# Delta-rule attention and two MoE layers on one core: both halves of each attention stage together, TensorE held in program order, PSUM divided anew, sums stored in four transfers

## The chip, the core and the metric

One core of one Trainium2 chip runs the whole program. The metric is device microseconds of one execution, the median of the runs. Engines in the profile: PE is TensorE, DVE is VectorE, ACT is ScalarE, POOL is GpSimd, SP is SyncE, which here issues DMAs only. PSUM is the memory that PE writes; ACT and DVE read results out of it.

## The reference

Three layers one after the other. The first is a delta-rule attention: per batch and head a 48x48 state is read and corrected token by token over 768 tokens. Its output feeds two mixture layers on 3072 tokens.

```python
B, H, S, D = 4, 8, 768, 48
for t in range(S):
    y[:, :, t] = einsum('bhd,bhde->bhe', q[:, :, t], state)
    v_old = einsum('bhde,bhd->bhe', state, k_n[:, :, t])
    state = state + beta[:, :, t] * einsum('bhd,bhe->bhde', k_n[:, :, t], v[:, :, t] - v_old)
x = y.transpose(0, 2, 1, 3).reshape(3072, 384)
h = maximum(x @ w_in, 0); x = (h * h) @ w_out          # 384 -> 2048 -> 384
h = maximum(maximum(x @ w1, x @ w2), x @ w3)           # 384 -> 768
out = h @ w_out2                                       # 768 -> 384
```

## The kernel before

**Chunks.** The 768 tokens are cut into 12 chunks of 64. Within a chunk the recursion is written as products of small matrices and one triangular inverse per head and batch; from chunk to chunk only the state `Sb` is carried. Each matrix product with float32 weights is done as three products of a high and a low part (`xh`, `xl`; `gh`, `gl`; `win_h`, `win_l`).

**Main loop.** Before it stands a prologue (Gram products and the inverses of the first two chunks). Then 12 rounds follow, one for each chunk `c`. In round `c`, `moe_a(c)` does the first mixture layer of chunk `c`: eight groups `s1` (18 matmuls into `p`, 2 PSUM buffers, then relu and square on ACT, the cast `gh` on ACT and the difference `gl` on DVE) and eight groups `s2` (12 matmuls into `px`). `s2` of a group stands two groups behind its `s1`, so that the last two `s2` groups close the round. The columns of `px` beyond the 384 sums also take a part of the attention's sums. At the end two DVE transposes bring `px` to SBUF as `xs`, and DMAs on SP's queue store it to `x2_d[c]`, eight for each chunk.

**Woven in.** `steps` takes a step of other generators between the steps of `moe_a`, each at a rate of its own: `attention(c+1)`; `kkps` in rounds 1, 3, 5, 7 (Gram products of two later chunks: PE `pk`, `pq`, DVE mask products, stores `kk`, `p` on SP's queue); `solve32` in rounds 0, 2, 4, 6, 8 (a load `buf<-kk`, then a chain of some 60 vector operations on DVE from `ss` at L247 over the pairs L268 and L270 to L271, which inverts two chunks' triangles; `norm` transposes a factor on PE as `pt`).

**Attention.** The 16 pairs of batch and head pair are split in two halves `p` = 0 and 1. For each half: `st0` multiplies `v` by `normT` (L419), forms `pA` and `pY` from the state and takes `r = v - pA` (L434); `zz` and `ww` (both halves at once, `pZ`, `pW`) finish the inverse; `mm_u` gives `pU`, copied to `u`; `st2` gives the output `pY` and the state's growth `pD` (then `Sb`), copied to `yy`; `st3` transposes `yy` on PE (`pT`) to `xh` and `xl` of chunk c+1. All of these matmuls address quarters or sixteenths of the array (64x64, 48x64 or 32x32), while `p` and `px` use 128x128.

**Order.** The kernel is written with Tile: a scheduler orders every engine's instructions by its own model of times from the order in which they are emitted, their dependences, and extra ordering edges (`behind`). The program of PE is therefore not in the order of the code; the split stages that the next section but one shows are the scheduler's. Phase 3 (the second mixture layer, from 655.46 us) follows the last round.

## Time and profile before

| what | value |
|---|---|
| runs | 960.38, 962.7, 967.49 us, median 962.7 us |
| profiled execution | 961.26 us, of which the span of the profile 959.5 us and 1.76 us around it |
| PE busy | 892.2 us, 93% of the span |
| DVE, ACT, POOL busy | 470.4, 409.2, 149.3 us |
| rounds 0 to 11 | 80.20 to 655.46 us |
| phase 3 | 655.46 to 959.5 us |

The profiled execution lies 1.4 us under the median. Times in the views are counted from the start of the span. A round begins where its first `p` matmul begins.

### The profile page before, as it was taken

To read this page: it belongs to the slowest core of one execution; us is meant where nothing else is said; L and a number is where in the kernel's file an instruction comes from. 1 tells how busy PE (TensorE), PEld (TensorE's weight loads), DVE (VectorE), ACT (ScalarE), POOL (GpSimd) and SP (SyncE) were. 2 spreads that over 40 slices of the span, in tenths; PEclk is the share of its full clock that TensorE was granted. 3 is DMA by queue.
4 is the path that set the end of the run, shared out by engine and by line. 5 is a ranking of instruction groups with operands and counts; after the bars stand their busy time and mean duration, and the time that the engine had idled before them with its cause. 6 is when DMAs were issued, how large, how long until landed. Compare 5 with 4: busy or idle time off the path is not lost.

```text
span 959.5 us, 26517 instructions
## 1 busy us (share of the span) xinstructions
PE 892.2 (93%) x11422; PEld 855.0 (89%) x11422; DVE 470.4 (49%) x1048; ACT 409.2 (43%) x857; POOL 149.3 (16%) x245
## 2 busy tenths in 40 slices
PE   5438889889999999999999999999999999999998
PEld 4337778889999999999999999999999999999998
DVE  2978886249424942493258354466623323323221
ACT  1756854444454545444544466473422212212211
POOL 2351112310322142214211420001100000000000
PEclk8557979999999999999999999999999999999999
DMA  9977723571574156426532633234301100100000
GB/s 198 336 207 188 213 69 81 154 170 55 145 188 93 56 150 179 99 61 161 149 74 69 144 112 101 59 100 110 114 25 33 42 25 25 33 21 14 17 17 34
DMA packets 118309, 98.83 MB, mean 103 GB/s; under 512 B 76160, under 2 KB 98480, under 8 KB 118192
## 3 DMA queue, kind: packets, MB, share of 16 engines
q1 hardware_dynamic: 97408, 58.23, 23.3%
q0 software_dynamic: 11712, 32.41, 12.5%
q10 hardware_dynamic: 9072, 6.49, 2.3%
q8 instruction: 90, 1.47, 0.7%
q14 instruction: 27, 0.22, 0.1%
HBM read 72.45 MB, written 24.64 MB: 101 GB/s over the span
## 4 chain that ended last, share of the span: by engine, by line
PE 80%; DVE 11%; ACT 4%; DMA 3%; issue 2%; SPq 0%; ACTq 0%; DVEq 0%
PE p L909 23%; PE p L548 20%; PE px L566 18%; PE po L926 8%; DVE buf L270 3%; DVE buf L268 3%; PE pA L429 2%; PE pU L446 2%; PE pY L493 1%; DVE gl L555 1%; DMA buf<-kk 1%; PE pD L471 1%; PE pT L514 1%; PE pk L180 1%; PE pY L429 1%
## 5 line engine op out<-in xcount | busy, mean ns | idle before, releaser
L909 PE MATMUL p<-x_h,w 128*128 128x384 f32 x864 | 220.1, 336 | 0.0
L566 PE MATMUL px<-wout,gh 128*128 128x384 f32 x768 | 202.6, 343 | 2.6 <-ACT wout L126 1.2
L548 PE MATMUL p<-xh,win_h 128*128 128x256 f32 x576 | 168.7, 294 | 5.7 <-DVE gl L555 4.5
L548 PE MATMUL p<-xl,win_h 128*128 128x256 f32 x576 | 164.2, 288 | 1.5 <-DVE xl L518 1.3
L548 PE MATMUL p<-xh,win_l 128*128 128x256 f32 x576 | 164.3, 286 | 0.0
L909 PEld LDWEIGHTS p<-x_h,w 128*128 128x128 f32 x864 | 156.2, 188 | 0.1
L909 PE MATMUL p<-x_l,w 128*128 128x384 f32 x432 | 145.3, 336 | 0.0
L566 PEld LDWEIGHTS px<-wout,gh 128*128 128x128 f32 x768 | 135.6, 189 | 6.1 <-ACT wout L126 1.4
L555 DVE TENSOR_TENSOR gl<-p,gh 128x512 fp32r<-128x512 f32 x96 | 66.2, 689 | 143.0 <-ACT gh L554 143.0
L566 PE MATMUL px<-wout,gl 128*128 128x384 f32 x384 | 130.1, 339 | 0.0
L548 PEld LDWEIGHTS p<-xh,win_h 128*128 128x128 f32 x576 | 111.1, 193 | 9.7 <-issue 2.6
L548 PEld LDWEIGHTS p<-xl,win_h 128*128 128x128 f32 x576 | 110.8, 194 | 2.7 <-DVE xl L518 2.0
L548 PEld LDWEIGHTS p<-xh,win_l 128*128 128x128 f32 x576 | 111.5, 194 | 0.3
L552 ACT ACTIVATE p<-p 128x512 f32<-128x512 f32 x96 | 55.9, 582 | 130.1 <-PE p L548 128.8
L915 DVE TENSOR_TENSOR mx<-p,mx 128x384 f32<-128x384 f32 x48 | 26.7, 557 | 123.0 <-PE p L909 123.0
L909 PEld LDWEIGHTS p<-x_l,w 128*128 128x128 f32 x432 | 81.3, 188 | 0.0
L917 ACT CAST hh<-mx 128x384 fp32r<-128x384 f32 x48 | 24.6, 513 | 119.4 <-DVE mx L916 119.3
L566 PEld LDWEIGHTS px<-wout,gl 128*128 128x128 f32 x384 | 72.3, 188 | 0.8 <-DVE gl L555 0.2
L554 ACT CAST gh<-p 128x512 fp32r<-128x512 f32 x96 | 56.3, 587 | 17.1 <-PE px L566 14.7
L270 DVE TENSOR_TENSOR buf<-buf 128x30 f32<-128x30 f32 (+9 forms) x180 | 60.6, 337 | 5.5
L268 DVE TENSOR_TENSOR buf<-buf 128x30 f32<-128x30 f32 (+9 forms) x180 | 60.0, 333 | 5.5
L553 ACT ACTIVATE p<-p 128x512 f32<-128x512 f32 x96 | 55.9, 582 | 2.9
(183 smaller groups left out, 1372.0 us busy)
## 6 DMA issues: line engine op xcount, KB each, us to landing
kq<-in_kc_dram POOLq DMA_DIRECT2D x22, 448.0 KB, 4.9
raw<-in_moe_w_dram SPq DMA_DIRECT2D x18, 384.0 KB, 3.4
p<-p POOLq DMA_DIRECT2D x22, 256.0 KB, 3.2
raw<-in_moe_w_out_dram SPq DMA_DIRECT2D x13, 384.0 KB, 3.4
v<-in_vt_dram POOLq DMA_DIRECT2D x24, 192.0 KB, 4.5
ktp<-in_kt_dram POOLq DMA_DIRECT2D x24, 192.0 KB, 3.0
x<-xs SPq DMA_DIRECT2D x96, 48.0 KB, 2.6
out_dram<-os ACTq DMA_DIRECT2D x24, 192.0 KB, 1.9
```

The costliest lines, as they stand in the source:

```text
L268: eng.tensor_tensor(out=tv, in0=M[:, 0:j, j].unsqueeze(2).broadcast_to([u, j, m]), in1=M[:, j, j + 1:n].unsqueeze(1).broadcast_to([u, j, m ...
L270: yield eng.tensor_tensor(out=M[:, 0:j, j + 1:n], in0=M[:, 0:j, j + 1:n], in1=tv, op=ALU.add)
L429: j = pe.matmul(ps[half(t ^ i), u], kq_[feat(t), u, i], Sb[feat(t), U2 * p + u], start=not i or u == 0, stop=not i, skip_group_check=bool(i))
L548: pe.matmul(p1[:, j], w[:, k, f], x[c][:, k], start=n == 0 and j == 0, stop=n == 8, skip_group_check=True)
L552: act.activation(out=p1, in_=p1, func=AF.Relu)
L553: act.activation(out=p1, in_=p1, func=AF.Square)
L554: last_gh[0] = act.copy(gh, p1).ins
L555: last_gl[0] = vec.tensor_sub(out=gl, in0=p1, in1=gh.bitcast(F32)).ins
L566: g = pe.matmul(px[:, h, 0:DM], x[:, j, hs], w, start=f == 0 and i == 0, stop=f == NF - 1 and i == 2, skip_group_check=True)
L909: pe.matmul(p, w[i][:, k, fs], x[:, k], start=n == 0, stop=n == 8)
L915: vec.tensor_max(out=t, in0=ps[1], in1=t)
L926: pe.matmul(po[:, 0:DM], x[:, f, js], w[:, f], start=i == 0, stop=i == 17)
```

## The change

**Halves.** From chunk 1 on, each of `st0`, `mm_u`, `st2`, `st3` does both halves in one step, where a half had steps of its own; the rate of the attention's steps falls with their number. `load_att` of both halves of the next chunk is issued after `st2`.

**Order on PE.** From round 2 on, each matmul and transpose goes through `tc.keep_in_program_order`, so that the scheduler keeps PE's instructions in the order in which the code emits them.

**PSUM.** `ps_at` (for `pA`, `pU`, `pD`, `pZ`, `pW`, `pT`, Gram products) has 2 buffers where it had 3; `ps_y` (for `pY`) has 2 where it had 1. `r` is no tile of its own: the subtraction writes `v`. `yy` has 2 buffers.

**Copies.** For half 1 (all chunks but chunk 1) the copies of `u` and `yy` out of PSUM are put on DVE instead of ACT.

**Stores.** `store_sums` stores `xs` by four DMAs of twice the size, at the second `s1` group of the next round. `x2_d` gets an axis for the halves of a chunk's 256 tokens; phase 3 loads `xr` by 128 tokens (twelve DMAs for a block of 384 tokens instead of eight, each run of bytes half as long). The transposes to `xs` stay behind the last DVE copy of the attention.

**Numbers.** The step at which the inverse is put after its load (`landing`) is 14 in round 2; `norm` comes at step 24 instead of 12; the Gram products begin later.

```diff
-    ps_at = pp.enter_context(tc.tile_pool(name="ps_at", bufs=3, space=PSUM))
-    ps_y = pp.enter_context(tc.tile_pool(name="ps_y", bufs=1, space=PSUM))
+    ps_at = pp.enter_context(tc.tile_pool(name="ps_at", bufs=2, space=PSUM))
+    ps_y = pp.enter_context(tc.tile_pool(name="ps_y", bufs=2, space=PSUM))
...
+        def matmul(self, *a, **k):
+            i = nc.tensor.matmul(*a, **k)
+            return tc.keep_in_program_order(i) if self.ordered else i
...
-            r = fresh("r", p, 6, [128, U2, D])
-            vec.tensor_sub(out=r, in0=v, in1=pA)
+            vec.tensor_sub(out=v, in0=v, in1=pA)
...
+            on_vec = p and c != 1
+            def put(to, po):
+                if on_vec:
+                    last_vec[0] = vec.tensor_copy(to, po).ins
+                else:
+                    last_act[0] = act.copy(to, po).ins
...
-                    if p and not c:
+                    if p and c != 1:
                         last_vec[0] = vec.tensor_copy(yy[p][half(i), :, t], pY[half(1 - t), Q * i:Q * i + Q]).ins
...
-            order = ((st0, 0),), *(((),) if c in (4, 10) else ()), ((zz, (k21, x1)),), *(((),) if c == 1 else ()), ((ww, 0),), ((mm_u, 0),), ((st2, 0),), ((st0, 1), (st3, 0)), ((mm_u, 1),), ((st2, 1),), ((st3, 1),)
+            order = both(st0), ((zz, (k21, x1)),), *(((),) if c == 1 else ()), ((ww, 0),), both(mm_u), both(st2), both(st3)
...
-            vec.transpose(out=xs[:, h], in_=px[:, h, 0:DM])
-            for a in range(4):
-                nc.sync.dma_start(x2_d[c][:, :, 4 * h + a], xs[32 * a:32 * a + 32, h].rearrange("i (b j) -> i b j", j=32))
+            i = vec.transpose(out=xs[:, h], in_=px[:, h, 0:DM])
+            if last_vec[0]:
+                behind(i.ins, last_vec[0])
+        sums.append((c, xs))
...
+        c, xs = sums.pop()
+        for a in range(4):
+            nc.sync.dma_start(x2_d[c].rearrange("i h b a j -> a i (h b) j")[a], xs[32 * a:32 * a + 32].rearrange("i h (b j) -> i (h b) j", j=32))
...
-                if g and n == 12:
+                if g and n == (24 if g > 1 else 12):
                     norm(nm)
...
-                extra.append(((10 if c in (3, 9) else 9) / 15.0, attention(c + 1)) if c > 1 else (13 / 15.0, later(3, attention(1))) if not c else (16 / 15.0, later(5, attention(2))))
+                extra.append((6.8 / 15.0, attention(c + 1)) if c > 1 else (11 / 15.0, later(3, attention(1))) if not c else (14 / 15.0, later(6, attention(2))))
...
-                solve_next = solve32(SOLVE[c], landing=16 if c == 8 else 10) if c else solve32(1, (pool,) * 2)
+                solve_next = solve32(SOLVE[c], landing={2: 14, 8: 16}.get(c, 10)) if c else solve32(1, (pool,) * 2)
...
             if c == 2:
                 kc_after.clear()
+                pe.ordered = True
```

Three places show what becomes of the order. In the changed kernel every matmul has the line of the wrapper, L48.

PE in round 4, before: the products of `st2` of half 0 (`pY`, `pD`) in the middle, where an `s2` group stands between two parts of them.

```order
L471 MATMUL pD<-u,ktp_147 64x48 x2
L493 MATMUL pY<-u,p 64x48 x2
L566 MATMUL px<-wout_1069,gh 128x384 x2
L566 MATMUL px<-wout_1069,gl 128x384
L566 MATMUL px<-wout_1069,gh 128x384 x2
L566 MATMUL px<-wout_1069,gl 128x384
L566 MATMUL px<-wout_1069,gh 128x384 x2
L566 MATMUL px<-wout_1069,gl 128x384
L566 MATMUL px<-wout_1069,gh 128x384 x2
L566 MATMUL px<-wout_1069,gl 128x384
L471 MATMUL pD<-u,ktp_147 64x48 x2
L493 MATMUL pY<-u,p 64x48 x2
```

The run of half 0 is broken after a few products and taken up again after the twelve `px` matmuls. The same place, changed (`st2` of both halves).

```order
L48 MATMUL pY<-u,p 64x48 x2
L48 MATMUL pD<-u,ktp_147 64x48 x2
L48 MATMUL pY<-u,p 64x48 x2
L48 MATMUL pD<-u,ktp_148 64x48 x2
L48 MATMUL pY<-u,p 64x48 x2
L48 MATMUL pD<-u,ktp_148 64x48 x2
L48 MATMUL pY<-u,p 64x48 x2
```

The stage is one run: half 1 (`ktp_148`) follows half 0 (`ktp_147`) with no `s2` group in it. Counted over PE's whole order, a run of small products stands between two runs of `p` or `px` 14, 7, 10, 13, 11, 12, 11, 12, 11, 11, 11 times in rounds 0 to 10 before, and 12, 12, 9, 10, 6, 10, 6, 10, 6, 6, 6 times now (123 and 93).

DVE at the end of round 4, before, in two pieces of one stretch: first the `gl` of the round's eighth `s1` group (`p_4707`) among the operations of the inverse (L268, L270), ten rows further the end of the inverse (L271) and what follows it.

```order
L270 TENSOR_TENSOR buf<-buf 128x23x8
L268 TENSOR_TENSOR buf<-buf 128x168
L270 TENSOR_TENSOR buf<-buf 128x24x7
L555 TENSOR_TENSOR gl<-p_4707,gh 128x512
L268 TENSOR_TENSOR buf<-buf 128x150
L270 TENSOR_TENSOR buf<-buf 128x25x6
```

This `gl` stands 14 rows ahead of L271. The end of the stretch:

```order
L268 TENSOR_TENSOR buf<-buf 128x30
L270 TENSOR_TENSOR buf<-buf 128x30
L271 TENSOR_TENSOR buf<-buf,a_4138 128x1024
L582 STREAM_TRANSPOSE xs<-px 128x384 x2
L518 TENSOR_TENSOR xl<-pT,xh 128x3x128
L419 TENSOR_TENSOR v<-v,normT 128x384
L434 TENSOR_TENSOR r<-v,pA 128x384
```

Behind L271 come the `xs` transposes, then the `xl` and `v` of half 1 alone. The same stretch, changed (L281, L283 and L284 are the inverse, `p_4719` the eighth group of round 4, `p_4796` the first of round 5).

```order
L283 TENSOR_TENSOR buf<-buf 128x29x2
L281 TENSOR_TENSOR buf<-buf 128x30
L283 TENSOR_TENSOR buf<-buf 128x30
L570 TENSOR_TENSOR gl<-p_4719,gh 128x512
L284 TENSOR_TENSOR buf<-buf,a_4115 128x1024
L531 TENSOR_TENSOR xl<-pT,xh 128x3x128 x2
L433 TENSOR_TENSOR v<-v,normT 128x384 x2
L599 STREAM_TRANSPOSE xs<-px 128x384 x2
L570 TENSOR_TENSOR gl<-p_4796,gh 128x512
```

The `gl` is now the row ahead of L284, and both halves' `xl` and `v` come behind it. In round 6, changed, that `gl` (`p_6198`) stands behind L284.

```order
L281 TENSOR_TENSOR buf<-buf 128x30
L283 TENSOR_TENSOR buf<-buf 128x30
L284 TENSOR_TENSOR buf<-buf,a_5594 128x1024
L570 TENSOR_TENSOR gl<-p_6198,gh 128x512
L531 TENSOR_TENSOR xl<-pT,xh 128x3x128 x2
L433 TENSOR_TENSOR v<-v,normT 128x384 x2
L599 STREAM_TRANSPOSE xs<-px 128x384 x2
```

So the eighth group's `gl` went from the middle of the inverse's last part to its end (round 4) or behind it (round 6).

SP at the border of rounds 1 and 2, before: `kk` and `p` are stores of Gram products, `x_130<-xs` the stores of round 1's sums, `buf<-kk_98` the load that round 2's inverse begins with.

```order
L185 DMA kk_98<-buf 64x512 x2
L205 DMA p_110<-buf 64x512 x2
L584 DMA x_130<-xs 384x1x32 x8
L185 DMA kk_98<-big 64x512 x2
L205 DMA p_110<-big 64x512 x2
L287 DMA buf<-kk_98 32x32x32 x2
L167 DMA big<-in_kc_dram 112x1024
```

All eight stores of sums stand ahead of the last stores of Gram products. Changed:

```order
L198 DMA kk_98<-buf 64x512 x2
L612 DMA x_130<-xs 768x1x32 x3
L218 DMA p_110<-buf 64x512 x2
L198 DMA kk_98<-big 64x512 x2
L612 DMA x_130<-xs 768x1x32
L180 DMA buf<-in_kc_dram 112x1024
L180 DMA big<-in_kc_dram 112x1024
L218 DMA p_110<-big 64x512 x2
L300 DMA buf<-kk_98 32x32x32 x2
```

Of the four stores of sums three stand ahead of the last `kk` store now, and one behind it.

## Rows read from the trace of the kernel before

**Rows 1.** The page: PE's busy time, and the chain that ended last.

```profile
PE 892.2 (93%) x11422; PEld 855.0 (89%) x11422; DVE 470.4 (49%) x1048; ACT 409.2 (43%) x857; POOL 149.3 (16%) x245
...
PE 80%; DVE 11%; ACT 4%; DMA 3%; issue 2%; SPq 0%; ACTq 0%; DVEq 0%
```

**Rows 2.** Windows by round (0, 1, 4, 5, 8, 9, 10): stretch, length, busy PE, PEld, DVE, ACT, POOL, clock, DMA.

```profile
80.20:142.15 61.95, 54.92 (x739) 49.71 (x737) 52.26 (x132) 45.84 (x96) 7.57 (x12) 0.87 0.52 151
142.15:197.07 54.92, 48.79 (x922) 45.50 (x921) 26.05 (x59) 22.78 (x48) 15.54 (x26) 1.00 0.47 123
...
295.65:340.23 44.58, 44.58 (x698) 42.06 (x696) 33.94 (x91) 21.64 (x50) 6.99 (x11) 1.00 0.25 65
340.23:389.47 49.24, 48.79 (x953) 45.95 (x951) 14.04 (x26) 23.16 (x49) 15.56 (x26) 1.00 0.70 175
...
483.23:529.19 45.96, 45.05 (x697) 42.27 (x695) 34.47 (x93) 21.77 (x50) 6.99 (x11) 1.00 0.23 62
529.19:575.59 46.40, 45.61 (x697) 42.81 (x695) 19.24 (x40) 25.41 (x55) 15.73 (x26) 1.00 0.51 131
575.59:620.28 44.69, 44.13 (x590) 41.59 (x588) 21.19 (x43) 26.53 (x57) 0.00 (x0) 1.00 0.29 78
```

**Rows 3.** Timeline of PE: `st2` of half 0 in two parts, of half 1 in one.

```profile
410.50 0.26 PE L493 MATMUL pY<-u,p 64*64 64x48 f32 x2
...
410.98 0.62 PE L566 MATMUL px<-wout,gh 128*128 128x384 f32 x2
...
411.61 0.51 PE L566 MATMUL px<-wout,gh 128*128 128x384 f32 x2
...
412.13 0.51 PE L566 MATMUL px<-wout,gh 128*128 128x384 f32 x2
...
413.26 0.26 PE L471 MATMUL pD<-u,ktp 64*64 64x48 f32 x2
...
414.09 0.45 PE L566 MATMUL px<-wout,gh 128*128 128x384 f32 x1
...
428.31 0.26 PE L493 MATMUL pY<-u,p 64*64 64x48 f32 x2
...
429.39 0.45 PE L566 MATMUL px<-wout,gl 128*128 128x384 f32 x1
```

**Rows 4.** Timeline of DVE in round 4: start, duration.

```profile
307.27 0.18 DVE L247 COPY ss<-buf 128x32 f32<-128x32 f32 x1
...
307.73 1.46 DVE L419 TENSOR_TENSOR v<-v,normT 128x384 f32<-128x384 f32 x1
...
334.26 0.68 DVE L555 TENSOR_TENSOR gl<-p,gh 128x512 fp32r<-128x512 f32 x1
...
338.72 1.23 DVE L271 TENSOR_TENSOR buf<-buf,a 128x1024 f32<-128x1024 f32 x1
...
340.82 0.52 DVE L518 TENSOR_TENSOR xl<-pT,xh 128x384 fp32r<-128x384 f32 x1
```

**Rows 5.** Costliest groups on ACT and DVE: the copies of `yy`.

```profile
L508 ACT COPY yy<-pY 64x192 f32<-64x192 f32 x92 | 28.8, 313 | 29.1 <-PE pD L471 25.7 <-PE pY L493 2.4
...
L506 DVE COPY yy<-pY 64x192 f32<-64x192 f32 x4 | 1.4, 354 | 0.1
```

**Rows 6.** Timeline of SP's DMA issues and of DVE at the border of rounds 1 and 2.

```profile
196.94 5.56 SPq L584 DMA_DIRECT2D x<-xs  x8
...
212.57 0.19 DVE L247 COPY ss<-buf 128x32 f32<-128x32 f32 x1 [4.94 <-DMA buf<-kk]
```

**Rows 7.** Waits of PE in round 2: total, times, longest.

```profile
PE pt L260 <- DVE nm L222: 1.7, 1, 1.7
PE pW L407 <- ACT k L399: 1.1, 1, 1.1
```

**Rows 8.** Windows within round 2: columns as in rows 2.

```profile
216.00:218.00 2.00, 2.00 (x11) 2.00 (x11) 1.79 (x6) 1.10 (x6) 0.04 (x1) 0.50 0.28 69
218.00:220.00 2.00, 2.00 (x15) 2.00 (x14) 1.83 (x9) 0.31 (x1) 0.00 (x0) 0.73 0.03 5
```

More of the change, by code (lines that the diff above doesn't have):

```diff
@@ L68, in delta_moe @@
     xt_d = [dram.tile([2, 2, B * Q, 32, 32], F32, name=f"xt{c}", tag=f"xt{c}") for c in range(NC)]
-    x2_d = [dram.tile([32, DM // 32, 8, 32], F32, name=f"x2{c}", tag=f"x2{c}") for c in range(NC)]
+    x2_d = [dram.tile([32, 2, DM // 32, 4, 32], F32, name=f"x2{c}", tag=f"x2{c}") for c in range(NC)]
     after, abs_after, cast_after, raw_after, x_after, raws = [], [], [], [], [], []
@@ L374, in fresh @@
         def fresh(name, p, i, shape):
-            if name == "r" and p and not c:
-                t = pkp.tile(shape, F32, name="r1", tag="r1")
-            else:
-                t = att.tile(shape, F32, name=name, tag=name, bufs=1 if name == "r" else 2)
+            t = att.tile(shape, F32, name=name, tag=name)
             tiles[c, p][i] = t
@@ L439, in mm_u @@
             n = U2 - (0 if not c else 2 if p else 4)
-            over = None if not c else (pYs[p][:, U2 * D:U2 * D + 2 * D] if p else pxs[0][:, :, DM:DM + 2 * D])
-            over = over if not c else over.rearrange("p (u d) -> p u d" if p else "p b (u d) -> p b u d", d=D)
+            if c:
+                free = pYs[p] if p else pxs
+                over = free[0].rearrange("p (b n) -> p b n", b=1) if p else free[0]
+                over = over[:, :, DM:DM + 2 * D].rearrange("p b (u d) -> p b u d", d=D)
             order = [u for i in range(U2) for u in (i, n + i) if (i < n if u == i else u < U2)]
@@ L447, in mm_u @@
                     else:
[L448 removed]
+                        o = over[half(1 - t), (u - n) // 2, (u - n) % 2]
                         i = pe.matmul(o, x[half(t), u], r[half(t), u], start=False, stop=True, skip_group_check=True)
[L450 removed]
+                        for j in free[1:]:
                             behind(i.ins, j)
             u_ = fresh("u", p, 7, [128, U2, D])
[L453 to L456 removed]
+            on_vec = p and c != 1
[4 more added lines that the diff above has]
+                    last_act[0] = act.copy(to, po).ins
+            put(u_[:, 0:n], pU[:, 0:n])
+            if c:
                 for t in range(2):
[L458 to L460 removed]
+                    put(u_[half(t), n:U2].rearrange("p (b u) d -> p b u d", u=2), over[half(1 - t)])
         yy, pDs = {}, {}
@@ L489, in st2 @@
             if not c:
-                pY = (ps_at if p else ps_y).tile([128, U2, D], F32, name="pY", tag="at" if p else "y")
+                pY = sums_y(p)
             for u in range(U2):
@@ L498, in st2 @@
                 grown(p)
-            if p and not c:
-                yy[p] = pkp.tile([128, Q, 2, D], F32, name="yy1", tag="yy1")
-            else:
-                yy[p] = att.tile([128, Q, 2, D], F32, name="yy", tag="yy", bufs=1)
+            yy[p] = att.tile([128, Q, 2, D], F32, name="yy", tag="yy")
             for i in range(2):
                 for t in range(2):
-                    if p and not c:
+                    if p and c != 1:
                         last_vec[0] = vec.tensor_copy(yy[p][half(i), :, t], pY[half(1 - t), Q * i:Q * i + Q]).ins
@@ L530, in attention @@
                 f(*p) if f is zz else f(p)
-                if f is (mm_u if c else state) and p and c + 1 < NC:
+                if f is (st2 if c else state) and p and c + 1 < NC:
                     load_att(c + 1, 0)
+                    load_att(c + 1, 1)
             yield
@@ L571, in moe_a @@
             s1(fp)
+            if fp == 1 and sums:
+                store_sums()
             yield
@@ L581, in moe_a, with store_sums @@
         for h in range(2):
-            vec.transpose(out=xs[:, h], in_=px[:, h, 0:DM])
-            for a in range(4):
-                nc.sync.dma_start(x2_d[c][:, :, 4 * h + a], xs[32 * a:32 * a + 32, h].rearrange("i (b j) -> i b j", j=32))
-        yield
+            i = vec.transpose(out=xs[:, h], in_=px[:, h, 0:DM])
+            if last_vec[0]:
+                behind(i.ins, last_vec[0])
+        sums.append((c, xs))
+        if c == NC - 1:
+            store_sums()
+        yield
+    sums = []
+    def store_sums():
+        c, xs = sums.pop()
+        for a in range(4):
+            nc.sync.dma_start(x2_d[c].rearrange("i h b a j -> a i (h b) j")[a], xs[32 * a:32 * a + 32].rearrange("i h (b j) -> i (h b) j", j=32))
     def steps(main, *others):
-        due = [0.0] * len(others)
+        due = [rest[0] if rest else 0.1 * pe.ordered for _, _, *rest in others]
         for _ in main:
-            for i, (rate, g) in enumerate(others):
+            for i, (rate, g, *_) in enumerate(others):
                 due[i] += rate
@@ L595, in steps @@
                     next(g, None)
-        for _, g in others:
+        for _, g, *_ in others:
             for _ in g:
@@ L749, in delta_moe @@
         for n, (c, p) in enumerate(todo):
-            pg = grams(n, 1, at)
+            pg = grams(n, 1, (p1, at)[n % 2])
             if c:
```

42 lines of the change are left out of this document (22 added, 20 removed).

## Prediction

> **What bounds the kernel now.** I read the page first. PE is busy for 892.2 of 959.5 us, and 80% of the chain that ended last is PE [rows 1]. So time goes only where PE does nothing, or where it does something that costs it more than its columns. The windows by round come second [rows 2]: the reader is to set PE's busy time beside a round's length. In round 4 they are equal (44.58 and 44.58), and round 6 reads alike; round 5 is idle for 0.45 us (49.24 less 48.79; rounds 3 and 7 alike, two more), round 9 for 0.79, round 10 for 0.56, round 8 for 0.91, rounds 0 and 1 for 7.0 and 6.1. In the steady rounds there is thus little idle time to win; what can be won is in the way the small products are strewn among the large. DVE stands beside that: 33.94 of 44.58 us in round 4, where it solves a triangle, but 14.04 of 49.24 in round 5, which has no solve [rows 2]. The third view is PE's timeline, for the price of breaking a run of small products [rows 3], the fourth DVE's at the end of a solve [rows 4].
>
> **What a broken run costs.** `st2` of half 1 runs in one piece, from 428.31 to 429.39, 1.08 us. The same work of half 0 is split: 410.50 to 410.98 and 413.26 to 414.09, 0.48 and 0.83, together 1.31 [rows 3]. So 0.23 us go inside the pieces. The twelve `px` between the pieces took 2.28 us, from 410.98 to 413.26, while three of them in the middle, from 411.61 to 412.13, took 0.52, which is 2.08 for twelve [rows 3]; so going there and back costs 0.2 more. The bounds are 0.23 and 0.43 for each run that is saved; I take the upper end, because the split stages also leave half-filled ends that the row does not count.
>
> **Steady rounds.** In even rounds the order of PE has 6 such runs where it had 11. Five by 0.43 are 2.2 us (1.2 at the lower end). If nothing else waited, rounds 4, 6, 8 and 9 would take 44.58 - 2.2 = 42.4 us. Moving the products costs nothing by itself, since every one of them is still done; what it needs is that `u`, `yy`, `xb` are there in time, now that PE may not take other work instead. Between two stages stand one `s2` and one `s1` group, some 4 us by the 2.08 us for the twelve `px`, against 1.4 us for four copies of `yy` at 0.31 to 0.35 [rows 3, 5]: covered.
>
> **Round 9 and 10.** Neither has a solve or Gram products. Round 9 goes from 46.40 to 42.6 (the 42.4 and 0.2 for waits), -3.8; only 5 runs and its idle time, 2.0 to 3.0, at the lower end. Round 10: five runs and 0.56 idle, -2.7 [rows 2].
>
> **Rounds 3, 5, 7.** 13, 12, 12 runs become 10. The Gram products keep their four runs, and `pk`, `pq` now share two PSUM buffers with the attention's stages, so that a mask product on DVE must be done before the next stage may start. I take two or three runs and the idle 0.45, -1.3 each, -3.9 in all; the ends are -1.9 each and 0, if the two buffers take it all back.
>
> **The solve rounds 4, 6, 8.** Here the gain meets DVE. From `ss` at 307.27 to the end of L271 (338.72 + 1.23 = 339.95) DVE is occupied back to back for 32.7 us, and `ss` comes 11.6 us after the round's start at 295.65 [rows 2, 4]. Nothing in the change shortens the solve. What stands among it changes: `v` (1.46), one `r` and one `xl` (0.52 each by the `xl` row) go; in come the `u` copies of half 1 (288 columns, so 0.4 by the `xl` row's 384, and two small parts at 0.2 to 0.3, under the `yy` row's 0.354, so 0.9) and four `yy` by 0.354, 1.4 [rows 4, 5]. The balance is -0.2. With `ss` at 11.6 again, behind the third `s1` group as before, L284 ends at 11.6 + 32.5 = 44.1 us of the round. PE, in order, wants the last `s2` group at 42.4 less its 2.1, at 40.3. But the `gl` of the eighth group, which that `s2` reads, stood at 334.26, 4.5 us ahead of L271 [rows 4], and now stands directly ahead of L284 in round 4, one operation of the solve ahead in round 8, and behind L284 in round 6. It is done at 44.1 - 1.2 = 42.9 in rounds 4 and 8: PE waits 2.6 us, and the round ends at 42.9 + 2.2 = 45.1. In round 6 it is done at 44.1 + 0.6 = 44.7, and the round ends at 46.8. The queued `xl` and `v` behind it take another 2 us on DVE and are late for the first group of the next round by nothing, since that group begins with `xh`. So round 4 goes +0.5, round 6 +2.2, round 8 (45.96 before) -0.9: together +1.8, where 42.4 each would have been -7.8.
>
> **The clock.** [...] Solve rounds in all: +3.3.
>
> **Copies on both engines.** ACT is busy for 21.64 of 44.58 us in round 4, DVE for 33.94 [rows 2]; the copies of half 1 move from the freer engine to the fuller one, 2.3 us for a round. [...]
>
> **Rounds 1 and 2.** The eight stores of sums held SP's queue for 5.56 us, ahead of the last Gram stores, which could go only at 202.5; DVE waited 4.94 us for the load made from it, until 212.57 [rows 6], and PE 2.8 us behind that [rows 7]. Three larger stores stand there now. An issue was 0.7 us (5.56 / 8); for twice the size I allow 0.7 to 1.4, and take 0.7, the row that there is: 2.1 instead of 5.56, 3.5 us less. But the last Gram products are done later in the new order, behind thirteen of the eighteen `p` matmuls that begin round 2 (some 2.1 us: thirteen by 0.12, two thirds of a `px` step of 0.173, and half a run of 1.08). I take -1.4; the ends are -4.3 (the 2.8 us wait and the 1.5 of clock all gone) and +1.5. Round 1 has more runs (12 for 7), but they now stand apart with `p` work between, where they stood in a row and waited; I set one against the other.
>
> **Round 0** has two runs less, -0.9; its order is otherwise much as before, DVE is busy for 52.26 of 61.95 us with weights [rows 2], and I allow 3 us either way. Prologue, round 11 and phase 3: the loads of `xr` in shorter pieces are issued ahead, on a queue nobody waits for there; nothing.
>
> **Sum.** -0.9 - 1.4 - 3.9 + 3.3 - 3.8 - 2.7 = -9.4. On the profiled execution, 961.26 us, that is 951.9. This execution lies 1.4 us under the median of 962.7.
>
> **Rivals.**
> First, no late tail: DVE gets through the solve because ACT's share is lighter and `ss` starts earlier (the third `s1` group has less ahead of it). Then rounds 4, 6, 8 give -7.8 in place of +3.3: 951.9 - 11.1 = 940.8. For it speaks that PE in order reaches its groups earlier; against it, that 32.7 us of DVE work in a row have only 42.4 us to stand in. Chance 0.20.
> Second, the gain is given back: the two PSUM buffers take the gain of rounds 3, 5, 7 (+3.9), and the clock falls in rounds 4 and 8 too (+3.0): 958.8. For it speaks that both stalls are new and the clock's price is in the rows. Chance 0.25.
> Third, slower: PE in order waits at every one of the last five `gl` of a solve round, since DVE has two solve operations or four `yy` (1.4 us) ahead of each. Five by 1.4 in four rounds are 28 us, with the clock down in all four 6 more, less the 3.3 that I have: 982.6. It passes 972 from about 0.9 us for each. Against it: an `s2` group stands two groups behind its `s1`, with some 6 us of other large matmuls between for ACT's three steps and the `gl`. Chance 0.08.
> Fourth, the order doesn't pay at all because broken runs cost PE nothing that it would not spend anyway, and only the waits stay: 961 to 965. Chance 0.03, since rows 3 have it otherwise.
>
> **How the numbers follow.** My own case has 0.44 and goes from 947 to 957: the lower price of a run on some 25 runs is +5, no fall of the clock -1.5, and rounds 0 to 2 3 us either way. The range takes in the first and second rival, 940 to 961; the third and the far ends are left out. A measurement of this kernel can tell about 1% from no change: under 953.1 is faster, over 972.3 slower. Of my case some 0.34 lies under 953.1, with the first rival's 0.20 that is 0.54; slower 0.08 with the third; the rest, 0.38, within 1%.
>
> **What would show it.** Even rounds with 6 runs of small products, `st2` in one run of some 2 us. In rounds 4, 6, 8 a wait of PE for `gl`, 2.6, 4.4 and 2.6 us, ahead of the last twelve `px`, and the clock at half behind round 6's. Rounds 9 and 10 at 42.6 and 42.0 us, rounds 3, 5, 7 at 47.9. In round 2 three `xs` stores of together 2.1 us ahead of the last `kk` store. I am wrong if the waits for `gl` are absent, if a round 9 without solve doesn't get shorter by 2 us, or if round 5 has waits for `pk` or `pq`.

## The result and the profile after

The changed kernel takes 976.97 us (median of 6 runs, 970.51 to 980.6) against 962.46 us before (6 runs): 1.0146 times as long, 95% interval 1.0104 to 1.0188. The forecast was 951.9 us, 940 to 961. The profiled execution after has a span of 974.0 us, 14.5 more than before.

The page after, which answers to [rows 1]: PE does its work in less busy time than before (892.2), so the gain from whole runs is there; the time is in PE's idle stretches (29.4 us in rounds 2 to 10, where it was 6.4).

```profile
PE 887.3 (91%) x11422; PEld 860.4 (88%) x11422; DVE 497.2 (51%) x1118; ACT 386.9 (40%) x787; POOL 150.2 (15%) x245
```

The windows by round after (4, 5, 8, 9, 10; columns as in [rows 2]). Round 9 is busy for 42.55 us, which is the 42.4 of the forecast, but lasts 44.13; rounds 4 and 8 are idle for 4.2 and 4.5 us, where round 4 was not idle at all [rows 2].

```profile
303.43:351.16 47.73, 43.53 (x697) 42.01 (x697) 37.07 (x99) 19.47 (x43) 7.00 (x11) 0.98 0.24 64
351.16:401.04 49.88, 48.37 (x952) 46.33 (x951) 16.05 (x31) 20.69 (x42) 15.64 (x26) 0.98 0.65 169
...
500.20:547.47 47.27, 42.82 (x697) 41.25 (x697) 36.10 (x97) 19.54 (x43) 7.01 (x11) 1.00 0.23 61
547.47:591.60 44.13, 42.55 (x696) 41.34 (x695) 20.39 (x44) 22.26 (x46) 15.64 (x26) 1.00 0.52 139
591.60:635.41 43.81, 42.55 (x631) 41.42 (x631) 24.82 (x52) 25.00 (x53) 0.00 (x0) 1.00 0.28 74
```

The waits of PE after say what the idle time waits for (total, times, longest). Two of these three were not in the forecast, nor was round 2's share of the second.

```profile
PE px L48 <- ACT u L472: 12.4, 9, 1.6
PE px L48 <- DVE gl L570: 12.3, 4, 3.8
...
PE pW L48 <- DVE buf L281: 3.9, 1, 3.9
```

**The wait for `u`** is new in each of rounds 2 to 10. In round 4, PE's timeline shows `mm_u` ending with `pU`, the transpose `pt`, and then an `s2` group that stands still for a microsecond:

```profile
327.36 0.63 PE L48 MATMUL pU<-v,xb 64*64 64x48 f32 x16
328.22 0.28 PE L52 MATMUL pt<-ident,nm 128*32 128x128 f32 x1 [0.22 <-ACT u L472]
329.51 0.62 PE L48 MATMUL px<-wout,gh 128*128 128x384 f32 x2 [1.00 <-ACT u L472]
```

ACT's timeline at that place: two copies read what `mm_u` wrote into the columns of `px` beyond the sums, with a `gh` between. `px` goes on when the second ends, at 329.45.

```profile
328.19 0.32 ACT L472 COPY u<-px 64x192 f32<-64x192 f32 x1
328.53 0.59 ACT L569 CAST gh<-p 128x512 fp32r<-128x512 f32 x1
329.14 0.31 ACT L472 COPY u<-px 64x192 f32<-64x192 f32 x1
```

The matmul writes other columns than the copy reads, and here it waits all the same (1.00 us). Before, the scheduler had put `p` matmuls between `mm_u` and `px` (in round 4 from 315.2 to 316.7 us), and no wait of this kind stood in rounds 2 to 10 of the trace. The nine waits after are 1.0 to 1.6 us each; what would come of not waiting, no run here shows.

**The wait for `gl`** is the forecast one: 3.0 us in round 4, 3.8 in round 6, 2.6 in round 8 (2.6, 4.4 and 2.6 were forecast); to this come 2.9 in round 2, for which none was forecast. DVE in round 4 after, which answers to [rows 4]:

```profile
314.75 0.18 DVE L260 COPY ss<-buf 128x32 f32<-128x32 f32 x1
315.23 1.08 DVE L231 TENSOR_SCALAR s<-s 128x32 f32<-128x32 f32 x1 [0.30 <-ACT s L230]
...
340.25 1.46 DVE L519 COPY yy<-pY 64x192 f32<-64x192 f32 x4
...
347.90 0.68 DVE L570 TENSOR_TENSOR gl<-p,gh 128x512 fp32r<-128x512 f32 x1
348.50 1.22 DVE L284 TENSOR_TENSOR buf<-buf,a 128x1024 f32<-128x1024 f32 x1
```

From `ss` to the end of the solve it is 35.0 us, where it was 32.7 and I had worked out 32.5. Behind three of these waits the granted clock falls to 0.50, here behind round 4's (columns as in [rows 2]); behind round 6's it was 0.50 from 446 to 452 us, behind round 2's 0.50 from 252 to 254; behind round 8's it stayed at 1.00.

```profile
348.00:350.00 2.00, 1.36 (x7) 1.36 (x8) 2.00 (x3) 0.00 (x0) 0.00 (x0) 0.92 0.00 0
350.00:352.00 2.00, 2.00 (x9) 2.00 (x8) 2.00 (x5) 0.00 (x0) 0.00 (x0) 0.50 0.70 164
352.00:354.00 2.00, 2.00 (x15) 2.00 (x14) 0.54 (x2) 0.00 (x0) 1.71 (x3) 0.72 0.50 133
```

**The wait in round 2.** SP's timeline after, which answers to [rows 6]. The three `xs` stores take 1.98 us, as forecast. But two key loads of 448 KB each now stand ahead of the load `buf<-kk` of the triangles, which DVE's `ss` (the last line) waits for until 215.41, 9.7 us behind its first issue. PE then stands for 3.9 us ahead of `pW`, and the granted clock is 0.50 from 220 to 226 us.

```profile
197.39 1.98 SPq L612 DMA_DIRECT2D x<-xs  x3
199.47 1.23 SPq L218 DMA_DIRECT2D p<-buf  x2
200.79 1.18 SPq L198 DMA_DIRECT2D kk<-big  x2
202.02 1.28 SPq L612 DMA_DIRECT2D x<-xs  x1
203.40 0.58 SPq L180 DMA_DIRECT2D buf<-in_kc_dram  x1
204.08 0.38 SPq L180 DMA_DIRECT2D big<-in_kc_dram  x1
204.55 1.09 SPq L218 DMA_DIRECT2D p<-big  x2
205.75 1.55 SPq L300 DMA_DIRECT2D buf<-kk  x2
215.41 0.19 DVE L260 COPY ss<-buf 128x32 f32<-128x32 f32 x1 [4.59 <-DMA buf<-kk]
```

### The profile page after: what moved, and what is told of

The parts are those of the page before. It is cut to its first block, busy times and chain, and to the rows that moved or that the text cites. A ratio compares the mean times of both kernels' runs of the same rounds, so it can differ in the third digit from the quotient of the medians.

```text
span 974.0 us, 26514 instructions
## 1 busy us (share of the span) xinstructions
PE 887.3 (91%) x11422; PEld 860.4 (88%) x11422; DVE 497.2 (51%) x1118; ACT 386.9 (40%) x787; POOL 150.2 (15%) x245
## 5 line engine op out<-in xcount | busy, mean ns | idle before, releaser
L48 PE MATMUL px<-wout,gh 128*128 128x384 f32 x768 | 208.8, 352 | 14.5 <-ACT u L472 12.4
L48 PE MATMUL p<-x_h,w 128*128 128x384 f32 x864 | 220.2, 336 | 0.0
L48 PE MATMUL p<-xh,win_h 128*128 128x256 f32 x576 | 168.0, 292 | 1.2 <-DVE gl L570 1.1
L48 PE MATMUL p<-xh,win_l 128*128 128x256 f32 x576 | 165.4, 287 | 0.0
L48 PE MATMUL p<-xl,win_h 128*128 128x256 f32 x576 | 165.1, 287 | 0.1
L48 PEld LDWEIGHTS p<-x_h,w 128*128 128x128 f32 x864 | 156.2, 188 | 0.0
L48 PEld LDWEIGHTS px<-wout,gh 128*128 128x128 f32 x768 | 138.9, 194 | 18.5 <-ACT u L472 13.9
L48 PE MATMUL p<-x_l,w 128*128 128x384 f32 x432 | 145.2, 336 | 0.0
L48 PE MATMUL px<-wout,gl 128*128 128x384 f32 x384 | 132.9, 346 | 12.3 <-DVE gl L570 12.3
L48 PEld LDWEIGHTS p<-xh,win_h 128*128 128x128 f32 x576 | 112.6, 195 | 3.1 <-DVE gl L570 1.5
L48 PEld LDWEIGHTS p<-xh,win_l 128*128 128x128 f32 x576 | 112.5, 195 | 0.4 <-DVE win_l L125 0.3
L48 PEld LDWEIGHTS p<-xl,win_h 128*128 128x128 f32 x576 | 112.3, 195 | 0.6 <-DVE xl L531 0.3
L48 PEld LDWEIGHTS px<-wout,gl 128*128 128x128 f32 x384 | 74.7, 194 | 13.6 <-DVE gl L570 13.6
L48 PEld LDWEIGHTS p<-x_l,w 128*128 128x128 f32 x432 | 81.2, 188 | 0.0
L283 DVE TENSOR_TENSOR buf<-buf 128x30 f32<-128x30 f32 (+9 forms) x180 | 60.7, 337 | 5.4
L281 DVE TENSOR_TENSOR buf<-buf 128x30 f32<-128x30 f32 (+9 forms) x180 | 60.4, 335 | 5.5
```

The source lines that it names most:

```text
L48: i = nc.tensor.matmul(*a, **k)
L281: eng.tensor_tensor(out=tv, in0=M[:, 0:j, j].unsqueeze(2).broadcast_to([u, j, m]), in1=M[:, j, j + 1:n].unsqueeze(1).broadcast_to([u, j, m ...
L283: yield eng.tensor_tensor(out=M[:, 0:j, j + 1:n], in0=M[:, 0:j, j + 1:n], in1=tv, op=ALU.add)
```

## The experiments

Three theories stood at the start: (1) `px` waits for ACT to read `mm_u`'s sums out of the buffer it writes, (2) the eighth `gl` of a solve round stands behind the solve, (3) the load of round 2 stands behind two key loads. The rival to all three was that holding PE in program order is itself the cost. e1, e8, e2, e4, e6 and e6b are the changed kernel with one edit. e3 has two: besides moving the loads it starts the program order on PE in round 4 instead of round 2. e7, e5, e12, e14 and e15 are built on e3's edit, so in all six PE is in the scheduler's order in rounds 2 and 3. Ratios are to the kernel before, measured beside each. To compare the rounds I take the time from the first `gh` of a round to that of the next, read off ACT's timeline (us):

| kernel | 2 | 3 | 4 | 5 | 6 | 7 | 8 | 9 | 10 |
|---|---|---|---|---|---|---|---|---|---|
| before | 49.8 | 49.6 | 44.7 | 49.1 | 44.7 | 49.1 | 46.0 | 46.4 | 44.3 |
| changed | 54.9 | 49.1 | 48.6 | 49.0 | 50.1 | 49.0 | 47.6 | 44.1 | 43.5 |
| e1 | 51.1 | 48.4 | 45.1 | 48.0 | 45.1 | 48.0 | 44.9 | 44.3 | 41.9 |
| e3 | 46.2 | 50.7 | 48.6 | 49.0 | 50.3 | 49.0 | 47.6 | 44.1 | 43.4 |
| e4 | 49.3 | 51.9 | 46.1 | 52.1 | 46.3 | 51.8 | 46.2 | 43.8 | 42.5 |
| e6b | 49.8 | 54.8 | 43.9 | 55.0 | 43.8 | 55.2 | 47.6 | 44.1 | 43.2 |
| e8 | 55.8 | 47.9 | 43.3 | 52.7 | 49.2 | 47.9 | 49.1 | 43.0 | 42.4 |
| e12 | 45.6 | 49.8 | 42.8 | 48.0 | 45.7 | 48.2 | 46.5 | 43.1 | 42.4 |
| e15 | 45.2 | 49.9 | 42.8 | 48.0 | 43.1 | 48.0 | 42.7 | 44.0 | 42.4 |

**e1, `mm_u` ahead of `p`.**

```diff
+        def paced(g):
+            for n in range(1, 15):
+                if n in (2, 5, 7, 10, 12, 14):
+                    next(g, None)
+                yield
...
-                extra.append((6.8 / 15.0, attention(c + 1)) if c > 1 else (11 / 15.0, later(3, attention(1))) if not c else (14 / 15.0, later(6, attention(2))))
+                extra.append((1.0, paced(attention(c + 1))) if c > 1 else (11 / 15.0, later(3, attention(1))) if not c else (14 / 15.0, later(6, attention(2))))
```

> The steps of the attention come one by one at fixed places of the round, so that mm_u is followed by an s1 group (p) and not by an s2 group (px). The work is the same. Theory (the first px behind mm_u must wait until ACT has copied the sums that mm_u put into px): the waits of px for ACT's u, 12.4 us in nine rounds of the changed kernel, fall under 2 us, and rounds 9 and 10, which have no solve, become 1.2 to 1.5 us shorter each (44.1 to 42.6 us, 43.8 to 42.6). DVE's order changes with it: the eighth gl stands ahead of the last six or more operations of the solve, so the waits of px for gl (12.3 us) fall too, and the time is 950 to 958 us. Rival (program order as such is the cost, PE meets the same late engine one place further on): the waits turn up at st2 or at p, round 9 stays over 43.8 us, and the time is 970 us or more.

956.28 us, ratio 0.9944 (0.992 to 0.9968): 0.6% under the kernel before by the edit of one schedule, PE still in program order. The waits of `px` for `u` are gone, those for `gl` fall from 12.3 to 4.9 us. Round 10 loses 1.6 us (1.2 expected); round 9 doesn't, because there `pZ` waits 0.7 us around the load of round 8's inverse, and `pW` 0.6. So theory 1 holds, but the edit also let the scheduler put the eighth `gl` ahead of the solve's end, and this run can't price (1) alone. e8 does that:

**e8, no sums in `px`.** Half 0's `mm_u` keeps all in `pU`; nothing else.

```diff
-            n = U2 - (0 if not c else 2 if p else 4)
+            n = U2 - (2 if c and p else 0)
...
-            if c:
+            if c and p:
```

> mm_u of half 0 keeps all its sums in pU, none in px; the steps stand where the changed kernel has them, mm_u directly ahead of an s2 group. Theory (the first px behind mm_u waits only because ACT must read the sums out of the buffer that px writes): the waits of px for ACT's u (12.4 us in nine rounds) are gone, mm_u itself takes 0.1 to 0.4 us more, rounds 9 and 10 become 1.0 to 1.4 us shorter, and the time falls from 977 to 962 to 968 us; the waits for gl stay within 3 us of 12.3 unless DVE's order moves. Rival (PE waits for ACT's u wherever it is read, at st2 or at the next group): the same wait shows at pY or p, time 974 us or more.

969.61 us, ratio 1.0079 (1.0052 to 1.0106); against the changed kernel 7.4 us less, where 9 to 15 were expected. The waits of `px` for `u` are gone, and rounds 9 and 10 each lose 1.1 us: theory 1 is shown where no solve stands. In the solve rounds only part of it came back: with `px` free PE meets the solve instead (`gl` 4.6 us at the longest, and 3.0 us at `pZ` in round 5, which needs the solve's result; there the scheduler had put the `gl` of round 4 far ahead of the solve's end, and the solve ended 5.2 us into round 5).

```profile
PE px L48 <- DVE gl L570: 11.8, 4, 4.6
...
PE pZ L48 <- issue: 3.0, 1, 3.0
```

Some 2.5 of the 7.4 us come from rounds 0 and 1, where the same sums stand in `px`: by first `p` the two take 116.8 us together instead of 119.3, and took 116.9 before the change.

**e3, the load first.** The last line, `pe.ordered = True`, stood under `c == 2`; behind the four new lines it stands under `c == 4`.

```diff
             if c == 2:
                 kc_after.clear()
+            if c == 3:
+                kc_after[:] = loaded
+            if c == 4:
+                kc_after.clear()
                 pe.ordered = True
```

> The two loads of keys for round 3 (448 KB each), which stand ahead of the load of round 2's triangles on SP's queue, are ordered behind it; nothing else. Theory (the load waits for their bytes: issued at 205.75, landed at 215.4): the load lands 4 to 5 us earlier, PE's wait of 3.9 us ahead of pW goes, and round 2 becomes 4 to 6 us shorter, 58.2 to 53 us; time 970 to 973 us. Rival (the load waits for the last store of Gram products, as before the change): it lands within 1.5 us of 215.4 and the time stays at 975 to 979 us.

969.23 us, ratio 1.007 (1.0044 to 1.0096), 7.7 us less than the changed kernel. SP's timeline: the key loads now stand behind `buf<-kk`.

```profile
203.20 1.18 SPq L198 DMA_DIRECT2D kk<-big  x2
206.21 0.31 SPq L300 DMA_DIRECT2D buf<-kk  x1
206.62 1.16 SPq L218 DMA_DIRECT2D p<-big  x2
207.83 0.58 SPq L300 DMA_DIRECT2D buf<-kk  x1
208.50 0.68 SPq L180 DMA_DIRECT2D buf<-in_kc_dram  x1
```

DVE's `ss` comes 6.3 us behind the first issue instead of 9.7:

```profile
212.50 0.19 DVE L260 COPY ss<-buf 128x32 f32<-128x32 f32 x1 [1.45 <-DMA buf<-kk]
```

But "nothing else" is not so: rounds 2 and 3 are out of program order as well. PE's order shows it: 13 runs of small products in round 2 instead of 9. Round 2 loses 8.7 us, its waits for `u` and `gl` among them, and round 3 gives 1.5 back. e4, further down, parts the two: it frees the order in both rounds and leaves the key loads ahead. Rounds 2 and 3 take 104.0 us in the changed kernel, 101.2 in e4 and 96.9 in e3 (table): 2.8 us come with the free order, some 4.3 with the place of the loads (3.6 by first `p`). In e4 the load goes out at nearly the same time as in e3, but `ss` comes 1.8 us later, and PE's wait ahead of `pW` is 3.1 us (3.9 in the changed kernel, 0.6 in e3):

```profile
214.27 0.19 DVE L260 COPY ss<-buf 128x32 f32<-128x32 f32 x1 [3.98 <-DMA buf<-kk]
```

So theory 3 holds, at some 4 us and not at 7.7.

**e2, the copies back on ACT.**

```diff
-            on_vec = p and c != 1
+            on_vec = p and not c
```

and the same for `yy`.

> The copies of u and yy of half 1 go back to ACT (2.3 us of DVE work less in each of the rounds 2 to 10). Theory (it is the place of the eighth gl behind the end of the solve, and not the amount of DVE's work, that makes PE wait): the end of the solve comes some 2 us earlier, but the gl stands directly behind it in all four rounds, so the waits of px for gl fall only from 12.3 to 8 to 11 us, those for u stay (12 us or more), and the time is 970 to 976 us. Rival (the amount of DVE's work): each of the four waits loses 2.3 us, 12.3 to 3, the half clock behind them goes, and the time is 960 to 966 us.

968.4 us, ratio 1.0066 (1.0044 to 1.0088): 8.6 us less, between the two. The waits for `gl` are 8.8 us as theory 2 had it (the `gl` stands behind the solve in all four rounds), but behind rounds 4 and 6 the clock of 0.50 is gone as the rival had it: from 345 to 347 us PE is busy for 0.73 of 2 us and goes on at 1.00, and behind round 6 the clock is 1.00 from 440 to 444 us. The fall stays behind round 2 (0.50 from 250 to 252 us) and is new behind round 8 (the last line).

```profile
345.00:347.00 2.00, 0.73 (x4) 0.73 (x5) 2.00 (x4) 0.00 (x0) 0.00 (x0) 1.00 0.30 66
347.00:349.00 2.00, 2.00 (x16) 2.00 (x15) 1.77 (x5) 0.00 (x0) 0.82 (x2) 1.00 0.73 197
...
538.00:540.00 2.00, 2.00 (x8) 2.00 (x7) 0.83 (x2) 0.00 (x0) 0.68 (x1) 0.51 0.89 194
```

The solve got 2.0 to 2.6 us shorter in all four rounds (32.5 instead of 35.0 us in round 4); in rounds 2, 4 and 8 some 0.6 of that is the `gl`, which no longer stands ahead of its end. So the amount of DVE's work matters as well as the order.

**e4, PE in no fixed order.** `pe.ordered = True` is left out.

> PE is not held in program order; all else as changed. The scheduler then puts two or eighteen p matmuls between mm_u and the next px, splits st0 in every round, and st3 stands further from the end. Theory (waits behind mm_u and for gl make the loss, not the order as such): with two p matmuls between, a wait of some 1.2 us stays in rounds 2 to 7, in rounds 8 to 10 (eighteen) none; together 6 to 8 us instead of 12.4; the waits for gl stay in the rounds whose gl stands behind the end of the solve (4, 6, 8); split stages cost 0.4 us each; time 966 to 974 us. Rival (program order is the cause of the loss): the time comes back to within 3 us of the kernel before, 960 to 965 us.

971.42 us, ratio 1.0099 (1.0069 to 1.0129): 5.5 us less than the changed kernel, 8.7 more than the kernel before. The scheduler takes most waits away: PE is idle for 11.2 us in rounds 2 to 10 instead of 29.4, `px` waits 1.0 us for `u` and 2.2 for `gl`. But there are 124 runs of small products again instead of 93, `st0` in several parts among them, and PE is busy 12.4 us longer than in the changed kernel (887.3) over the whole execution:

```profile
PE 899.7 (93%) x11422; PEld 864.4 (89%) x11422; DVE 497.2 (51%) x1118; ACT 388.7 (40%) x787; POOL 149.8 (15%) x245
```

The rival falls: without the order the time is not that of the kernel before, and e1 is under it with the order kept. The theory's own numbers were off (6 to 8 us of waits expected, 1.0 found).

**e6 and e6b, `gl` ahead of the solve's end.** The last six pairs of the solve and its end are emitted later, behind the eighth `gl`, in rounds 2, 4, 6 (the expectations count eight and seven pairs; `n >= 24` of 30 makes six). In e6 the transpose `pt` was moved with them.

```diff
+                if g > 1 and n >= 24:
+                    behind(i.ins, last_gl[0])
                 ops.append(i.ins)
+                if g > 1 and n == 23:
+                    for _ in range(18):
+                        yield
-                if g and n == (24 if g > 1 else 12):
+                if g and n == (22 if g > 1 else 12):
```

> In rounds 2, 4 and 6 the last eight pairs of operations of the solve are held behind the eighth gl on DVE (round 8's order stays, its gl behind the end); the same work on every engine. Theory (the place of gl): the waits of px for gl in these three rounds (2.9, 3.0, 3.8 us) fall under 0.7 us each, round 8's stays at 2.6 or more, no half clock behind rounds 2, 4 and 6, and the time falls by 10 to 14 us, to 963 to 967 us. Rival (DVE has too much to do in a solve round): the wait moves to the first p of the next round, which needs xl, or to the next solve's start, and the time falls by less than 4 us.

e6: 980.23 us, ratio 1.0188 (1.0149 to 1.0228). The three waits for `gl` went and `pt` waited 7.4 us for `xl`: my edit's own fault. The last two lines above are e6b's:

> The run before (e6) held the last pairs of the solve behind the eighth gl, but with that also moved the transpose pt to the end of the round, where it waited for xl to free a PSUM buffer (7.4 us), so that it told nothing on the sum. Here pt stands two pairs earlier, ahead of the held part. In this build round 2, 3rd and 2nd solve round (4 and 6) have gl seven pairs ahead of the end of the solve, round 8 keeps it one operation ahead. Theory (the place of gl): no wait for gl over 0.7 us in rounds 2, 4, 6, one of 2.3 to 3 us in round 8, no wait of pt for xl, time 963 to 968 us. Rival (DVE has too much to do in a solve round): the waits move to the start of the next round (p for xl, px for gl), time 972 us or more.

e6b: 980.92 us, ratio 1.0192 (1.0152 to 1.0232). In rounds 4 and 6 the waits are gone and the rounds are 4.7 and 6.3 us shorter; rounds 5 and 7 are 6.0 and 6.1 us longer. The rival won. What took it back is seen in round 5, first on DVE and SP (the solve ends at 351.87, 4.7 us into the round, and the `xs` stores go ahead of its store `xt`), then on PE, where `pZ` needs the load of `xt`, which POOL issues from 356.98 to 361.89. The second `pZ` row names that load; the 2.72 us of the first the profile puts down to nothing ("issue"). Behind it the granted clock is 0.50 from 366 to 370 us, which adds to the price (in the changed kernel a 128x256 `p` matmul took 0.42 us at 351.16, where the clock was 0.50, and 0.28 at 570.67, where it was 1.00).

```profile
350.64 1.23 DVE L284 TENSOR_TENSOR buf<-buf,a 128x1024 f32<-128x1024 f32 x1
```

```profile
350.04 2.67 SPq L612 DMA_DIRECT2D x<-xs  x4
352.81 3.20 SPq L321 DMA_DIRECT2D xt<-buf  x4
```

```profile
364.27 0.28 PE L48 MATMUL pZ<-xb,k 32*32 32x32 f32 x2 [2.72 <-issue]
364.73 1.07 PE L48 MATMUL pZ<-xb,k 32*32 32x32 f32 x62 [0.18 <-DMA xb<-xt]
```

So theory 2 falls as it stood. A solve round has two ends on DVE, the `gl` that this round's last `s2` reads and the end of the solve that the next round's `pZ` reads; here, putting one first made the other late. From `ss` to the end it was 37.3 us here, in round 4, with `xl`, `v` and `xs` among the last operations.

**e7, e1 and e3 together.**

> The attention's steps at fixed places (mm_u ahead of p) and the two key loads behind round 2's load, both together. Theory (the two losses lie in different rounds and add up): the first alone gave 956.3 us, the second alone took 7.7 us off the changed kernel, so 948 to 951 us, with PE's wait of 4.5 us ahead of pW in round 2 gone. Rival (the solve of round 2 ends late either way, and round 3 waits for its later loads): 953 to 957 us.

955.67 us, ratio 0.9938 (0.9917 to 0.9959), no better than e1 alone beyond its spread: the rival. Round 2 lost 2.5 us, rounds 3 and 9 gave 1.6 back; rounds 2 and 3 differ from e1 in PE's order as well as in the loads, and which of the two costs round 3 its 0.8 us no run shows.

**e5, e7 with the copies on ACT; e12, e8 with e3 and the copies on ACT.**

> Attention's steps at fixed places (mm_u ahead of p), the two key loads behind round 2's load, and the copies of half 1 back on ACT. Theory (in a solve round and the one behind it the end is set by the chain ss, solve on DVE, store xt, load xb, pZ, and every DVE operation among the solve lengthens it): without the 2.3 us of copies the span from ss to the end of the solve falls from 34.7 to some 32.5 us, the last waits of px for gl (5.5 us) and pT for yy fall, rounds 4 to 7 become 1 to 2 us shorter for each pair, and the time is 948 to 952 us against 955.7 with the copies on DVE. Rival (the copies on ACT now delay the products p that ACT reads, or gl stands behind the solve in round 2 again): 955 to 959 us.

954.91 us, ratio 0.9911 (0.9877 to 0.9946). The solve takes 31.1 to 31.9 us, shorter than expected, but the waits for `gl` grow to 7.6 us, since the scheduler again puts it at the solve's end: no gain that can be told from e7.

> As the run before in copies and loads, but the steps stand where the changed kernel has them, and mm_u of half 0 writes nothing into px. Theory (with px free and 2.3 us less on DVE both the wait for u and the length of the solve are gone, so the place of mm_u matters no more): waits of px for u 0, from ss to the end of the solve under 33.5 us, waits of px for gl 3 to 6 us in the rounds with gl behind the end of the solve; 950 to 957 us. Rival (the attention's place in the round decides by itself, since pZ and pW come earlier or later against the load xb): 960 us or more, with waits at pZ.

950.25 us, ratio 0.9871 (0.9846 to 0.9896), inside what the theory gave. Round 4, where `gl` by itself stands twelve operations ahead of the solve's end, takes 42.8 us; rounds 6 and 8, where it stands behind the end, 45.7 and 46.5.

**e14, e12 with the sums stored as before.**

```diff
-        sums.append((c, xs))
-        if c == NC - 1:
-            store_sums()
+        for h in range(2):
+            for a in range(4):
+                nc.sync.dma_start(x2_d[c][:, h, :, a], xs[32 * a:32 * a + 32, h].rearrange("i (b j) -> i b j", j=32))
```

> The best version so far (e12, 950.25 us) with the sums stored as in the kernel before: eight small transfers at the end of each round instead of four at the second s1 group of the next. Theory (the stores matter in one place, on SP's queue ahead of the last Gram store of round 2, and are hidden elsewhere): the eight stores hold the queue there for 5 to 5.6 us instead of 2.7, ss of round 2 comes 2 to 3.5 us later, round 2 is 2 to 3.5 us longer and the others are alike: 952 to 954 us. Rival (the stores are hidden everywhere, the load of round 2 is held by other things): 949 to 951.5 us.

951.06 us, ratio 0.989 (0.9855 to 0.9924), the rival: `ss` of round 2 comes at 208.09 instead of 207.76. With the load ahead of the key loads, and round 2 in the scheduler's order as in e12, four or eight stores make no difference; `ss` waits for no load there in either.

**e15, e12 with `gl` ahead of the solve's end in each solve round.** As e6b, but for the last three pairs and the end only (`n >= 27`), and for round 8 too.

> e12 with the eighth gl ahead of the last ten or so operations of the solve in rounds 2, 6 and 8 too, as it stands in round 4 by itself; xl and v then stand among the last operations. Theory (in a solve round the wait for gl and the late end of the solve are two prices of the same DVE time: with 2.3 us less on DVE the second has room again): the waits of px for gl (4.6 us) go, rounds 6 and 8 become 2 to 3 us shorter, rounds 7 and 9 at most 1 us longer, time 945 to 949 us. Rival (as in e6b the late end of the solve takes it back at pZ of the next round): 949 to 953 us with waits at pZ.

943.85 us, ratio 0.982 (0.9793 to 0.9848): 1.8% under the kernel before, and the best. No wait of `px` for `gl` is left, and `pZ` waits for a solve's result in round 9 alone, 0.2 us. Nearly the same order that cost as much as it gave in e6b pays here. From `ss` to the end of the solve it is 33.2 to 34.5 us against 36.9 to 38.2 in e6b's rounds 2, 4, 6: 2.3 us of copies are gone from DVE, and `xs` stands behind the end. That the copies decide is not shown. In e1, with the copies on DVE and `gl` ten operations ahead of the end, the solve takes 35.9 us in rounds 4 and 6, and rounds 5 and 7 last 48.0 us as they do here. What the runs do show is when the end is too late: up to 2.5 us into the next round (e1, e15) `pZ` waits at most 0.7 us; 4.4 to 5.2 us into it (e6b, and round 5 of e8) it waits 2.7 to 3.1. What the free order in rounds 2 and 3 adds or takes here no run shows; round 3 lasts 49.9 us, and 47.9 in e8.

## Why the prediction was wrong

By first `p`, the terms of the sum against what was measured (us):

| part | forecast | measured |
|---|---|---|
| prologue and round 0 | -0.9 | +3.6 |
| rounds 1 and 2 | -1.4 | +4.6 |
| rounds 3, 5, 7 | -3.9 | +0.8 |
| rounds 4, 6, 8 | +3.3 | +9.3 |
| round 9 | -3.8 | -2.3 |
| round 10 | -2.7 | -0.9 |
| round 11 and phase 3 | 0 | -0.6 |

**Steady rounds: right in PE's own time.** Whole runs of small products give what was worked out: round 9 is busy for 42.55 us where 42.4 was forecast, and rounds 4, 6, 8 and 10 of e15, where the waits are gone, last 42.4 to 43.1.

**The step that failed first** is "covered" in the same part: "what it needs is that `u`, `yy`, `xb` are there in time". I asked who reads `u` next, not who writes the buffer that it is read from. `mm_u` leaves a part of its sums in `px`, and in program order an `s2` group stands right behind it: 12.4 us in nine rounds (forecast: 0). e8 shows it alone in rounds 9 and 10, 1.1 us each.

**Rounds 1 and 2** were to lose 1.4 us; together they grew by 4.6 (from 103.93 to 108.52, by the starts of rounds 1 and 3). The stores on SP's queue did as forecast (1.98 us), and in e14 four or eight of them made no difference. The step missed what else came ahead of the load, the two key loads that I had seen in the order of SP and not priced: some 4 us, by e3 against e4. It also gave round 2, a solve round too, no wait for `gl` (2.9 us) and none for `u` (1.5).

**The solve rounds' balance** of -0.2 us was mis-sized by 2.5: in round 4 the solve took 35.0 us instead of 32.5. The copies that came in, less `v`, `r` and `xl`, come to +0.1 instead of -0.2. I subtracted the 1.46 us of `v` [rows 4] in full. It had stood beside the mask that POOL makes behind `ss` (from 307.53 for 1.26 us); with `v` gone, an operation of the size of `ss` (0.18 us) takes 1.08 there (L231). That is 0.9 of the 2.5. DVE also waits for ACT, 0.30 us ahead of L231 and 0.56 for the `gh` at 335.91, where it had waited 0.17: some 0.8 more with what stands around it. The rest, about 0.5, I can't assign.

The mechanism, `gl` late at the end of a solve round and PE waiting in order, was right. That its size was right to 0.6 us is luck: in round 4 the `gl` was done 2.2 us later in the round than worked out (45.1, not 42.9), and PE, held up by `u`, wanted it 1.9 us later (42.2, not 40.3). The lengths of the rounds don't share the luck: 47.7, 49.4 and 47.3 us where 45.1, 46.8 and 45.1 were worked out.

**The clock** fell to 0.50 behind the waits of 2.9, 3.0 and 3.8 us in rounds 2, 4 and 6 and stayed at 1.00 behind the one of 2.6 in round 8. The +3.3 of the forecast holds 1.5 us for it, for round 6 alone; none was put in for rounds 2 and 4. No run shows that term: it was an estimate from the clocks in [rows 8], and what a fall costs is measured nowhere by itself. What the runs show in its place is the clock and the longer matmul, 0.42 us at 0.50 where it was 0.28 at 1.00.

**Rounds 3, 5, 7** were to lose 1.3 us each; by first `p` they went 49.6, 49.2, 49.2 to 49.1, 49.9, 49.8. The wait for `u` (1.5 us) and, in rounds 5 and 7, the clock of 0.50 at the start (to 352 and to 452 us) account for it: without either, rounds 5 and 7 take 48.0 in e15, 1.2 less than before, and round 3 takes 47.9 in e8. The two PSUM buffers cost nothing that can be seen: no `pk` or `pq` waits in these rounds.

**Round 0** began 3.4 us earlier and ended 3.6 later, with a wait of 3.8 us of `pY` for ACT's `u`; at its end that is 4.5 us off my -0.9. The forecast had nothing for the 3.4 us of the prologue; the change also lets its Gram products take turns between two PSUM tiles (`grams(n, 1, (p1, at)[n % 2])`), which the list of changes leaves out, and no run tries it apart. For round 0 itself e8 bears on the cause: with half 0's sums out of `px` the wait for `u` falls to 1.9 and 0.7 us, and round 0 takes 64.1 instead of 69.0 us, while round 1 takes 2.4 more. The scheduler's order moves with it, so by what path stays open.

**Rivals.** The slower one came out by time (over 972) but not by its mechanism: in the solve rounds no `gl` but the eighth was waited for. Of the second, the clock fell in round 4 (0.50) and not in round 8 (1.00), and the PSUM buffers took nothing. The first, no late tail, gave 940.8 (its -7.8 for rounds 4, 6, 8 is -7.9 by [rows 2]); e15, which has none, takes 943.85.

Copies on both engines did not pay in the solve rounds of the changed kernel: e2 takes the copies off DVE and gains 8.6 us, 6.8 of them in rounds 2, 4, 6 and 8 by first `p`. In e5 against e7 the same move gains nothing that can be told.
